# First stage of a Fourier mixer kernel: finer steps, a new hand-written order, fewer filler matmuls

## The chip, the cores and the metric

The kernel runs on one core of a Trainium2 chip. The metric is the device time of one execution in microseconds (us), the median of several runs. The core's engines are named as in the profile: PE (TensorE, matmuls), PEld (its weight loads), DVE (VectorE), ACT (ScalarE), POOL (GpSimd) and SP (SyncE, which here only issues DMAs).

## What is computed

Three layers, in 32-bit floats, for 4 batches of 768 rows with 512 columns:

```python
# 1. attention in chunks of 32 rows, 8 heads of 64, 8 memory keys beside a window of 56 keys
scores = scale * q_c @ k_full.T ; a = exp(scores - max) ; a = a / (sum(a) + 1e-9) ; out = a @ v_full
# 2. Fourier mixing and a dense layer
u  = x + real(fft(fft(x, axis=1), axis=2))
un = (u - mean(u)) / sqrt(var(u) + 1e-6)
x  = u + relu(un @ w_ch1) @ w_ch2              # 512 -> 2048 -> 512
# 3. gated convolution
h  = relu(x @ w_in)                            # 512 -> 1024
out = (h * sigmoid(conv3(h))) @ w_out          # 1024 -> 512
```

The weights come as 64-bit floats and are decoded on the chip to a high and a low 32-bit part; products of the large matrices are three matmuls each (high by high, high by low, low by high).

## The kernel before, in words

The program is one function whose steps are issued in an order that a string of letters, `SCHED` (L38), writes out by hand. A letter is one step, and `task` (L549) issues all its instructions on their engines at once; every engine then works through its own instructions in that order. `SCHED` has three parts, divided by `|`. Everything up to the end of part 3 is called the first stage here.

A *unit* is 96 rows of one batch, so there are 32 units, 8 to a batch. Its letters in part 1 are: `S` scores (L224, eight pairs of matmuls into the PSUM tile `sc`; then, in the same step, eight row maxima on DVE, `sm` and `ngm`, L240, and the load of the unit after next, L216); `E`, for half the heads, four exponentials on ACT (L248); `A`, for half the heads, four transposes on PE (`atp`, L257) and the copy out of PSUM (`at`, L163 or L161); `P` the product with the values (`o`, L268), then on DVE the denominators (`r`, L270, L271) and the scaled output (`xn`, L273), then on POOL the sums and differences of mirrored columns (`xf`, L278, L279); `X` four transposes on PE (`xtp`, L293) and the copy into the batch's rows `xT` (L296, L298). The scores use two PSUM buffers, one unit's worth, so the next unit's scores wait for this unit's row maxima.

`B` is one step of the Fourier transform of a batch (`dft`, L304), which can start when the batch's eight units are there: folding (`EO`, L309, L310, POOL; `F` and its high and low parts `Fhl`, L323 to L328), products with the tables (`z`, `p`, `pm` on PE), results `G` and `H` on DVE, their sum and difference `uc` (L462, L463), and the split into `uh` and `ul` (L477, L480). `D` is one step of the dense layer of a transformed batch (`dense`, L497): four of sixteen columns of the hidden layer, `h` (12 matmuls, L488; `hh` on ACT, `hl` on DVE), and the product `y` (12 matmuls, L507). `W` is one step of decoding a weight piece (`decode_all`, L105), mainly on DVE (`wsc`, `wlb`, `whb`). Which of two engines does a copy, a sum or a difference is written down for each instance in `ENGINES` (L39).

`F` is a filler: `keep(1)` (L204) multiplies a constant matrix with itself into a PSUM buffer that nobody reads (`idle`; one 32-bit product of 128 columns, which the profile counts as two matmuls).

The Fourier tables are loaded by POOL's queue in one go when the ninth `E` is issued (L563 to L566). After the first stage a loop of its own alternates `h` and `acc` products for the rest of the dense layer, then comes the third layer; neither is touched by the change apart from line numbers.

Of the kernel before, what the change touches and what calls it, by code (L numbers as in the profile page):

```python
# [37 lines left out]
SCHED = "FFFSEAEFSAWFWFFFEEPFFFSFFAFFWWAEPAFXSWFEAWESFFEWWPSFFEFFWXXAAEWWPEAFFSEFFFWAPAFFFEAXFEPAAFFFSFFFFFFWEFEXWPAASWXEWEPAXFFSFFBAPEEAXASFEBPSFAEBBFEFFFWBASEBXPXABASFEBWEBPAESFAWBBXBEPAAEESFBBBWBWXPASFBEABBWWBBBBXPEASFWXEAFFBWWPBEBEWASEBBAXEWPXAAFBSFEBBWEPSABBAWBWEXEDDWDWDPSAABEXDPDBBEBBBDABDAXESBBPDBEEBBXBABSDXBABPSEBBADBBABDPABDEBSEAXBBEBBEEPBSBABXBADBDEBBPEXABASDPBDADBDBBSXEXBDABESBPEABEABDBBSPBADFBBFEBXAEESDBBBBPABABBXDEPDBBAAEBXEBBBXBDBPADABDBPXDDXBB|BBBWDWBDWBBDWBDDDBBWWWBBWDDWBBBBWDWBWWDBDBWBWBWWWBWDWBWDDWWBWBBBWBBDBDBWDDBWBB|DDWDDWWDWWWWWDDWWWDWWHDWHDHDWHDWWWDDDWDWWWWWWW"  # L38
ENGINES = {'at': 'aaaaaaaaavavaaaaaaaaaaaaaaaaaaaaaaaaaaaaaaaaaavaaaavaaavaaaaaaaa', 'xt': 'vvvvaaaaaaaaaaaaavaaaaaaaaavaava', 'y': 'aaaaaaaaaaaaaaaaaaaaaaaaaaaaaaaa', 'uh': 'aaaaaaaaaaavavvvvaaavvaaavavaaaaaaaaaaavvv', 'ul': 'vvpvvvvvvvvvvvvpvvvvvvvvvpvvpppppvpvvvpppv', 'fl': 'pvvvvppvppvvppvp', 'f': 'vpvvvpppvpvpvvpv', 'u0': 'vvvvvvvv', 'u1': 'vvvvvvvv'}  # L39
# [7 lines left out]
def fourier_mixer_kernel(ctx: ExitStack, tc: tile.TileContext, qk, vw, w1, w2, w_in, w_out, conv_w,  # L47
# [57 lines left out]
    def decode_all(todo, st=None):  # L105

        st, lo_of = st or fetch(todo[0][0]), None
        for i, (_, where, f, spill) in enumerate(todo):
# [3 lines left out]
            while placed(f) is False:  # L112
                if lo_of is not None:
                    lo_of()
                    lo_of = None
                yield
# [51 lines left out]
    def run(gen, n=1):  # L168
        for _ in range(n):
            if next(gen, "end") == "end":  # L170
                return False
        return True
# [30 lines left out]

    def keep(n):  # L204

        p = ps_g.tile([128, 512], F32, tag="g", name="idle")
        for _ in range(n):
            mm(p[:, 0:128], onesm, onesm, start=True, stop=True)  # L208

    NUNITS = NB * NU  # L210
    units = {}
    def load_qk(u):
        if u < NUNITS:
            t = ldp.tile([128, QW + KWD], F32, tag="qk", name="qk", bufs=2)
            units[u] = {"qk": t}
            nc.sync.dma_start(out=t, in_=qk[u])  # L216

    def load_v(u):
        if u < NUNITS:
            t = ldp.tile([128, VW], F32, tag="vw", name="vw", bufs=3)  # L220
            nc.sync.dma_start(out=t, in_=vw[u])
            units[u]["vw"] = t

    def scores(u):  # L224
# [18 lines left out]
        d["ex"], d["ngm"] = sm, ngm  # L243
# [7 lines left out]
    def atr(u, half):  # L251
        d = units[u]
        if half == 0:
            d["at"] = smp.tile([128, NH, QB], F32, tag="at", name="at", bufs=1)
        at = ps_g.tile([128, 4, QB], F32, tag="g", name="atp")
        for i in range(4):
            nc.tensor.transpose(at[:, i, :], d["ex"][:, 4 * half + i, :], ident_sb[:QB, :QB])  # L257
        copy("at", d["at"][:, 4 * half:4 * half + 4, :], at)

    def pv(u):  # L260
# [3 lines left out]
        r = smp.tile([QB, NH], F32, tag="r", name="r")  # L264
        o = ps_o.tile([128, 2, 512], F32, tag="o", name="o")
        oh = o[:QB, :, 0:VW // 2].rearrange("p b (h e) -> p b h e", e=HD + 1)
        for h in range(NH):
            mm(oh[:, h // 4, h % 4, :], at_sb[:, h, :], vw[:, h * (HD + 1):(h + 1) * (HD + 1)], start=True, stop=True)  # L268
        r4 = r.rearrange("p (b h o) -> p b h o", b=2, o=1)
        nc.vector.tensor_scalar(out=r4, in0=oh[:, :, :, HD:HD + 1], scalar1=1e-9, scalar2=None, op0=ALU.add)  # L270
        nc.vector.reciprocal(out=r, in_=r)  # L271
        xn = smp.tile([QB, DM + 1], F32, tag="xn", name="xn", bufs=1)
        nc.vector.tensor_tensor(  # L273
            out=xn[:, 0:DM].rearrange("p (b h e) -> p b h e", b=2, e=HD), in0=oh[:, :, :, 0:HD],
            in1=r4.to_broadcast([QB, 2, 4, HD]), op=ALU.mult)
        xf = smp.tile([QB, 2, 256], F32, tag="xf", name="xf")
# [5 lines left out]
    xTs = {}  # L282

    def xtr(u):
        d = units.pop(u)
        b, blk = divmod(u, NU)
        if blk == 0:
            xTs[b] = xtp.tile([128, 4, S + 1], F32, tag="xT", name="xT")
        xT = xTs[b]
        xf = d["xf"].rearrange("p a (m c) -> p (a m) c", c=128)  # L290
        p = ps_g.tile([128, 4, QB], F32, tag="g", name="xtp")
        for i in range(4):
            nc.tensor.transpose(p[:, i, :], xf[:, i, :], ident_sb[:QB, :QB])  # L293
# [10 lines left out]
    def dft(b):  # L304
# [3 lines left out]
        for sl, rv in ((slice(97, 385), slice(671, 383, -1)), (slice(0, 97), slice(768, 671, -1))):  # L308
# [3 lines left out]
            while NU * b + NU - 1 in units or count["X"] < NU * b + NU:  # L312
                yield "wait"
# [20 lines left out]
        def zstep(c, m):  # L334
# [5 lines left out]
            z = ps_g.tile([128, 512], F32, tag="g", name="z")  # L340
# [9 lines left out]
            accumulate(z[:sn, 0:nw], seq)  # L350
            zh = dfp.tile([97, 256], F32R, tag=f"zh{c % 2}{m}", name="zh")
# [6 lines left out]
            if c < 2:  # L358
                nc.vector.tensor_tensor(out=zn[:sn, 1], in0=z[:sn, 256:258], in1=zn[:sn, 0].bitcast(F32),
                                        op=ALU.subtract)  # L360
                ZN[c, m] = zn
            Z[c, m] = (zh, zl, sn)

        def part(c, n, zc):
            terms = []
# [53 lines left out]
        def center(hf, gs):  # L419
            ss = slice(hf * HALF, hf * HALF + HALF)  # L420
            pm = ps_g.tile([128, 512], F32, tag="g", name="pm")
            mm(pm[:, 0:HALF], onesm, gs, start=True, stop=True)  # L422
            for m in range(2):
                nc.vector.tensor_tensor(out=G[:, m, ss], in0=G[:, m, ss], in1=pm[:, 0:HALF], op=ALU.subtract)
            nc.scalar.copy(gs[0:1, :], pm[0:1, 0:HALF])
            nc.sync.dma_start(out=mud[b][:, ss], in_=gs[0:1, :])

        gs = summed(0)
        for c in (2, 3):
            for m in range(2):  # L430
# [6 lines left out]
        for m in range(2):  # L437
            zc = slice(128 * m, 128 * m + 128)
            p = ps_g.tile([128, 512], F32, tag="g", name="p")
            for c, o, n in ((2, 0, 194), (3, 256, 192)):  # L440
# [4 lines left out]
                accumulate(p[:, o:o + n], seq[-1:], start=False)  # L445
            pj = p.rearrange("p (r j) -> p j r", r=2)
# [11 lines left out]
            yield  # L458
        uc = dfp.tile([128, 4, S], F32, tag="Fhl", name="uc")
        for hf in range(2):  # L460
# [5 lines left out]
            yield  # L466
            yield from split_uc(2 * b + hf, uc[:, :, ss])
            if hf:
                bgb.append(dense(b))
# [14 lines left out]
    def g1(c, f):  # L484
        uh, ul = uhl[c]
        need(("1", f))
        p = ps_g.tile([128, 512], F32, tag="g", name="h")
        accumulate(p[:, 0:TC], split3([(w1h[f][:, k * 128:k * 128 + 128], w1l[f][:, k * 128:k * 128 + 128],  # L488
                                        uh[:, k], ul[:, k]) for k in range(4)]))
        hh = a1p.tile([128, TC], F32R, tag="hh", name="hh", bufs=NI)  # L490
# [542 lines left out]
```

## Time and profile before

| what | us |
|---|---|
| median of 3 runs (1019.08 to 1025.03) | 1019.93 |
| the profiled execution, whole | 1020.89 |
| its span, from first to last instruction | 1018.1 |
| first stage ends (first `acc` product) | about 348 |

The span is what the profile's rows cover; the profiled execution's own time is 2.8 us longer than its span. Rows of the profile give the busy time of engines, the waits, and the instructions in order of time; times in them count from the span's start.

### The profile page before, as it was taken

To read this page: it belongs to the slowest core of one execution; us is meant where nothing else is said; L and a number is where in the kernel's file an instruction comes from. 1 tells how busy PE (TensorE), PEld (TensorE's weight loads), DVE (VectorE), ACT (ScalarE), POOL (GpSimd) and SP (SyncE) were. 2 spreads that over 40 slices of the span, in tenths; PEclk is the share of its full clock that TensorE was granted. 3 is DMA by queue.
4 is the path that set the end of the run, shared out by engine and by line. 5 is a ranking of instruction groups with operands and counts; after the bars stand their busy time and mean duration, and the time that the engine had idled before them with its cause. 6 is when DMAs were issued, how large, how long until landed. Compare 5 with 4: busy or idle time off the path is not lost.

```text
span 1018.1 us, 16674 instructions
## 1 busy us (share of the span) xinstructions
PE 999.1 (98%) x6430; PEld 957.6 (94%) x6430; DVE 685.8 (67%) x1508; ACT 442.5 (43%) x923; POOL 214.9 (21%) x232
## 2 busy tenths in 40 slices
PE   7899999999999999999999999999999999999997
PEld 6888989999999999999999999999999999999996
DVE  4889956766988775767787775635357566465554
ACT  4687754664444423333333332212245454454442
POOL 1353251422400000102211000202013222222222
PEclk9999999999999999999999999999999999999999
DMA  6864532522437545575788972818543111010101
GB/s 198 264 185 138 182 105 78 164 72 81 129 100 235 179 152 194 187 182 125 174 201 224 199 183 83 148 49 164 159 123 115 52 69 56 1 62 1 62 1 62
DMA packets 63807, 130.86 MB, mean 129 GB/s; under 512 B 4919, under 2 KB 39199, under 8 KB 63503
## 3 DMA queue, kind: packets, MB, share of 16 engines
q1 hardware_dynamic: 51424, 102.35, 30.6%
q0 software_dynamic: 12048, 27.17, 14.9%
q8 instruction: 50, 0.82, 0.3%
q14 instruction: 29, 0.24, 0.1%
q10 hardware_dynamic: 256, 0.28, 0.1%
HBM read 92.28 MB, written 43.79 MB: 134 GB/s over the span
## 4 chain that ended last, share of the span: by engine, by line
PE 90%; DVE 5%; issue 2%; ACT 1%; DMA 1%; POOL 1%; DVEq 0%; POOLq 0%; ACTq 0%
PE acc L66 32%; PE h L66 25%; PE ph L66 12%; PE y L66 6%; PE o L268 3%; PE sc L234 2%; PE p L66 2%; PE z L66 2%; DVE sm L240 2%; PE atp L257 2%; PE idle L208 1%; PE xtp L293 1%; PE pm L422 1%; ACT sm L248 0%; DMA qk<-in_qk 0%
## 5 line engine op out<-in xcount | busy, mean ns | idle before, releaser
L66 PE MATMUL acc<-hh,w 128*128 128x384 f32 x768 | 208.0, 334 | 0.0
L66 PE MATMUL h<-uh,w 128*128 128x384 f32 x768 | 208.0, 334 | 0.0
L492 ACT ACTIVATE hh<-h 128x384 fp32r<-128x384 f32 x128 | 62.5, 490 | 247.2 <-PE h L66 247.1
L493 DVE SCALAR_TENSOR_TENSOR hl<-h,hh 128x384 fp32r<-128x384 f32 x128 | 70.5, 554 | 145.6 <-ACT hh L492 145.1
L66 PEld LDWEIGHTS acc<-hh,w 128*128 128x128 f32 x768 | 139.8, 188 | 0.0
L66 PEld LDWEIGHTS h<-uh,w 128*128 128x128 f32 x768 | 139.8, 188 | 0.0
L66 PE MATMUL ph<-xh,wit 128*128 128x384 f32 x512 | 136.3, 337 | 0.7 <-ACT hrow L823 0.7
L66 PE MATMUL acc<-hl,w 128*128 128x384 f32 x384 | 128.3, 334 | 0.0
L66 PE MATMUL h<-ul,w 128*128 128x384 f32 x384 | 128.3, 334 | 0.0
L66 PE MATMUL acc<-wot,hgh 128*128 128x512 f32 x384 | 119.6, 393 | 0.0
L831 DVE SCALAR_TENSOR_TENSOR cv<-hrow,cw_sb,cv 128x768 f32<-128x768 f32 x64 | 110.1, 1721 | 3.1 <-ACT cv L825 2.0
L843 POOL TENSOR_TENSOR hgl<-cv,hgh 128x768 fp32r<-128x768 f32 x32 | 60.4, 1886 | 194.6 <-ACT hgh L842 179.0
L837 DVE TENSOR_TENSOR cv<-hrow,cv 128x768 f32<-128x768 f32 x32 | 30.7, 959 | 99.2 <-ACT cv L836 99.1
L66 PEld LDWEIGHTS ph<-xh,wit 128*128 128x128 f32 x512 | 93.3, 188 | 2.6 <-ACT hrow L823 1.4
L66 PE MATMUL ph<-xl,wit 128*128 128x384 f32 x256 | 86.1, 336 | 0.0
L66 PEld LDWEIGHTS acc<-wot,hgh 128*128 128x128 f32 x384 | 71.7, 188 | 13.4
L248 ACT ACTIVATE sm<-sm,ngm 96x128 f32<-96x128 f32 x256 | 80.5, 394 | 7.4 <-DVE ngm L240 7.4
L823 ACT ACTIVATE hrow<-ph 128x384 f32<-128x384 f32 x64 | 31.3, 493 | 102.3 <-PE ph L66 101.1
L66 PE MATMUL acc<-wot,hgl 128*128 128x512 f32 x192 | 74.7, 389 | 0.0
L66 PEld LDWEIGHTS acc<-hl,w 128*128 128x128 f32 x384 | 72.1, 188 | 0.0
L66 PEld LDWEIGHTS h<-ul,w 128*128 128x128 f32 x384 | 72.1, 188 | 0.0
L240 DVE CUSTOM_DVE_ANT_0 sm<-sc,mask_sb 96x128 f32<-96x128 f32 x256 | 56.3, 282 | 18.3 <-PE sc L234 14.5
(150 smaller groups left out, 1879.2 us busy)
## 6 DMA issues: line engine op xcount, KB each, us to landing
w<-in_w SPq DMA_DIRECT2D x32, 512.0 KB, 4.1
qk<-in_qk SPq DMA_DIRECT2D x32, 448.0 KB, 3.5
us<-ucd SPq DMA_DIRECT2D x13, 768.0 KB, 7.9
yp<-yd SPq DMA_DIRECT2D x13, 768.0 KB, 8.4
vw<-in_vw SPq DMA_DIRECT2D x32, 260.0 KB, 3.0
ucd<-uc SPq DMA_DIRECT2D x8, 768.0 KB, 4.7
yd<-y SPq DMA_DIRECT2D x32, 192.0 KB, 2.0
ucd<-mud POOLq DMA_DIRECT2D x8, 768.0 KB, 14.4
```

The costliest lines, as they stand in the source:

```text
L66: mm(o, a, b, start=(start and i == 0), stop=(stop and i == n - 1))
L234: mm(sch[2 * a + g], qT[64 * g:64 * g + 64, a, :], kT[64 * g:64 * g + 64, a, :], start=True, stop=True)
L240: nc.vector.tensor_tensor_reduce(out=sm[:, h, :], in0=sch[h], in1=mask_sb[:, kind, :], op0=ALU.add, op1=ALU.min, scale=-0.125, scalar=3e38 ...
L248: nc.scalar.activation(out=d["ex"][:, h, :], in_=d["ex"][:, h, :], func=AF.Exp, scale=-1.0, bias=d["ngm"][:, h:h + 1])
L257: nc.tensor.transpose(at[:, i, :], d["ex"][:, 4 * half + i, :], ident_sb[:QB, :QB])
L268: mm(oh[:, h // 4, h % 4, :], at_sb[:, h, :], vw[:, h * (HD + 1):(h + 1) * (HD + 1)], start=True, stop=True)
L492: nc.scalar.activation(out=hh, in_=p[:, 0:TC], func=AF.Relu)
L493: nc.vector.scalar_tensor_tensor(out=hl, in0=p[:, 0:TC], scalar=0.0, in1=hh.bitcast(F32), op0=ALU.max, op1=ALU.subtract)
L823: nc.scalar.activation(out=h[:, 1 + hf * TC:1 + hf * TC + TC], in_=p[:, 0:TC], func=AF.Relu)
L831: nc.vector.scalar_tensor_tensor(out=cv, in0=h[:, j:j + S], scalar=cw_sb[:, j, f:f + 1], in1=cv, op0=ALU.mult, op1=ALU.add)
L837: nc.vector.tensor_tensor(out=cv, in0=h[:, 1:S + 1], in1=cv, op=ALU.mult)
L843: nc.gpsimd.tensor_tensor(out=hgl[i], in0=cv, in1=hgh[i].bitcast(F32), op=ALU.subtract)
```

## The change

Steps are cut finer, and the string is written anew. The row maxima become a step of their own in two halves (`T`); the copies out of PSUM are steps apart from the transposes (`a`, `x`); the denominators, the reciprocal and the scaled output are steps of their own (`p`, `r`, `n`); each load of a unit is a step (`l`, `v`); the tables come in five pieces (`t`). A `B` or `D` step is cut in two where its product has been issued and its result has not been read. `SCHED` has 13 `F` where it had 63, and 34, 24 and 29 `W` in its three parts where it had 33, 27 and 26. `ENGINES` is written anew as well. The assertions (`after`, `bank`, `taken`, `spent`) issue nothing, and `AHEAD` is empty.

```diff
-SCHED = "FFFSEAEFSAWFWFFFEEPFFFSFFAFFWWAEPAFXSWFEAWESFFEWWP
...
+SCHED = "FFWFvSTETSAlEWWlTATvWEaaWSTPEEAFaTApWSarEFlnPT
...
 def load_qk(u):
-        if u < NUNITS:
-            t = ldp.tile([128, QW + KWD], F32, tag="qk", name="qk", bufs=2)
...
+    def load_table(n):
+
+        if n in (0, 1):
+            nc.gpsimd.dma_start(out=dtab_sb[:, n], in_=dtab[:, n])
+        elif n == 2:
+            nc.sync.dma_start(out=sgn_sb, in_=sgn)
+            for row in (0, LOROW):
+                nc.gpsimd.dma_start(out=orow_sb[row:row + 1], in_=orow)
+        else:
+            nc.gpsimd.dma_start(out=stab_sb[:, n - 3], in_=stab[:, n - 3])
...
+    def rowmax(u, half):
...
-        for h in range(NH):
+        for h in range(4 * half, 4 * half + 4):
             nc.vector.tensor_tensor_reduce(
...
+    def denom(u):
...
         nc.vector.tensor_scalar(out=r4, in0=oh[:, :, :, HD:HD + 1], scalar1=1e-9, scalar2=None, op0=ALU.add)
+
+    def inverse(u):
+        r = units[u]["r"]
         nc.vector.reciprocal(out=r, in_=r)
+
+    def pv_out(u):
...
     def dense(b):
...
-                g1(c, f)
+                p = g1(c, f)
+                if f == NI - 1:
+                    spent_u.add(c)
+                yield "half"
+                g1_out(c, f, p)
                 yield
...
-            if n == 8:
-                nc.gpsimd.dma_start(out=dtab_sb, in_=dtab)
-                for row in (0, LOROW):
-                    nc.gpsimd.dma_start(out=orow_sb[row:row + 1], in_=orow)
-                nc.gpsimd.dma_start(out=stab_sb, in_=stab)
...
+        elif k == "T":
+            rowmax(n // 2, n % 2)
```

Three places show what moves. On PE at the start of the program, before (`sc` scores, `atp` and `xtp` transposes, `o` the product with the values, `idle` the fillers):

```order
L208 MATMUL idle<-onesm 128x128 x3
L234 MATMUL sc<-qk 96x128 x8
L257 MATMUL atp<-ident_sb,sm 128x96 x4
L208 MATMUL idle<-onesm 128x128
L234 MATMUL sc<-qk 96x128 x8
L257 MATMUL atp<-ident_sb,sm 128x96 x4
L208 MATMUL idle<-onesm 128x128 x4
L268 MATMUL o<-vw,at 96x65 x8
L208 MATMUL idle<-onesm 128x128 x3
```

and on PE at the same place in the changed kernel:

```order
L227 MATMUL idle<-onesm 128x128 x3
L281 MATMUL sc<-qk 96x128 x16
L315 MATMUL atp<-ident_sb,sm 128x96 x8
L281 MATMUL sc<-qk 96x128 x8
L331 MATMUL o<-vw,at 96x65 x8
L315 MATMUL atp<-ident_sb,sm 128x96 x4
L227 MATMUL idle<-onesm 128x128
```

The second unit's scores now stand ahead of the first unit's transposes, the third unit's ahead of the first product with the values, and of the eleven fillers of the first list four are left.

On DVE where the first unit's output is scaled, before (`r` denominators, `xn` the output, `wlb`, `wsc` and `rxb` the decoding of weights):

```order
L125 TENSOR_SCALAR wlb<-w_153 128x512
L129 SCALAR_TENSOR_TENSOR wlb<-w_153,wlb 128x512
L270 TENSOR_SCALAR r<-o 96x8
L271 RECIPROCAL r<-r 96x8
L273 TENSOR_TENSOR xn<-o,r 96x512
```

and on DVE at that place in the changed kernel:

```order
L340 TENSOR_SCALAR r<-o 96x8
L145 SCALAR_TENSOR_TENSOR rxb<-wlb,wsc 128x512
L129 TENSOR_SCALAR wsc<-w_204 128x512
L130 TENSOR_SCALAR wlb<-w_204 128x512
L344 RECIPROCAL r<-r 96x8
L351 TENSOR_TENSOR xn<-o,r 96x512
```

Weight steps now stand between the parts of what was one step.

On POOL where batch 0's transform ends (`gs` a sum of two halves of `G`, `xf` a unit's mirrored sums), before:

```order
L279 TENSOR_TENSOR xf<-xn 96x256
L416 TENSOR_TENSOR gs<-G 128x384 x2
L277 COPY xn<-xn 96x1
L278 TENSOR_TENSOR xf<-xn 96x256
L279 TENSOR_TENSOR xf<-xn 96x256
```

and on POOL at that place in the changed kernel:

```order
L509 TENSOR_TENSOR gs<-G 128x384
L356 COPY xn<-xn 96x1
L357 TENSOR_TENSOR xf<-xn 96x256
L358 TENSOR_TENSOR xf<-xn 96x256
L171 TENSOR_TENSOR uc<-G,H 128x2x384 x2
```

The two sums `uc` of the first half of batch 0, which DVE made before, are POOL's now, behind the mirrored sums of other units.

## Rows read from the trace of the kernel before

**Rows 1.** The page: busy time of each engine; PE's busy tenths in 40 slices

```profile
PE 999.1 (98%) x6430; PEld 957.6 (94%) x6430; DVE 685.8 (67%) x1508; ACT 442.5 (43%) x923; POOL 214.9 (21%) x232
...
PE   7899999999999999999999999999999999999997
```

**Rows 2.** Windows: stretch, length, PE, PEld, DVE, ACT, POOL busy (instructions), clock, DMA share, GB/s

```profile
0.00:60.20 60.20, 51.13 (x501) 45.79 (x502) 40.66 (x219) 37.21 (x106) 17.38 (x35) 1.00 0.73 226
60.20:117.80 57.60, 55.17 (x584) 50.25 (x583) 53.11 (x244) 45.05 (x134) 21.85 (x36) 1.00 0.53 159
117.80:348.00 230.20, 228.64 (x1720) 222.46 (x1719) 175.57 (x497) 117.50 (x297) 63.49 (x80) 1.00 0.38 124
348.00:1018.00 670.00, 664.21 (x3633) 639.11 (x3631) 416.45 (x550) 242.71 (x389) 112.19 (x82) 1.00 0.46 119
```

**Rows 3.** Windows of the fillers alone (tile idle): PE busy, PEld busy

```profile
0.00:60.20 60.20, 16.20 (x92) 13.40 (x92) 1.00 0.73 226
60.20:117.80 57.60, 6.04 (x30) 4.18 (x30) 1.00 0.53 159
117.80:348.00 230.20, 0.77 (x4) 0.67 (x4) 1.00 0.38 124
```

**Rows 4.** Timeline of PE: start us, length us, instruction, idle before it

```profile
1.09 1.65 PE L208 MATMUL idle<-onesm 128*128 128x128 f32 x6 [1.09 <-DVE expl L76]
5.05 2.02 PE L234 MATMUL sc<-qk 64*96 64x128 f32 x16 [2.31 <-DMA qk<-in_qk]
...
15.91 1.12 PE L234 MATMUL sc<-qk 64*96 64x128 f32 x16
...
47.73 1.83 PE L208 MATMUL idle<-onesm 128*128 128x128 f32 x14
49.40 0.49 PE L293 MATMUL xtp<-ident_sb,xf 96*128 96x96 f32 x4
...
60.18 0.49 PE L293 MATMUL xtp<-ident_sb,xf 96*128 96x96 f32 x4
...
117.78 0.42 PE L66 MATMUL h<-uh,rxa 128*128 128x384 f32 x1
```

**Rows 5.** Waits of DVE up to 117.8 us: total us, times, longest

```profile
DVE sm L240 <- PE sc L234: 13.4, 7, 6.1
DVE r L270 <- PE o L268: 4.6, 5, 1.6
```

**Rows 6.** Timeline of DVE: start us, length us, instruction, idle before it

```profile
7.10 0.29 DVE L240 CUSTOM_DVE_ANT_0 sm<-sc,mask_sb 96x128 f32<-96x128 f32 x1 [6.05 <-PE sc L234]
7.32 0.28 DVE L240 CUSTOM_DVE_ANT_0 sm<-sc,mask_sb 96x128 f32<-96x128 f32 x1
...
123.27 2.50 DVE L129 SCALAR_TENSOR_TENSOR wlb<-w,wlb 128x512 int32<-128x512 int32 x1
```

**Rows 7.** Groups of instructions by line: busy us, mean ns of one, idle before

```profile
L129 DVE SCALAR_TENSOR_TENSOR wlb<-w,wlb 128x512 int32<-128x512 int32 x48 | 36.1, 752 | 0.6
...
L166 POOL TENSOR_TENSOR ul<-us,uh 128x768 fp32r<-128x768 f32 x10 | 20.5, 2057 | 138.4 <-ACT uh L163 94.1 <-DVE uh L161 44.3
...
L166 DVE TENSOR_TENSOR uc<-G,H 128x768 f32<-128x768 f32 x16 | 14.5, 947 | 0.0
...
L166 POOL TENSOR_TENSOR F<-EO 128x576 f32<-128x576 f32 (+2 forms) x7 | 8.5, 1208 | 0.0
L166 POOL TENSOR_TENSOR Fhl<-F,Fhl 128x386 fp32r<-128x386 f32 (+1 forms) x8 | 8.4, 1055 | 19.4 <-ACT Fhl L325 19.4
L166 DVE TENSOR_TENSOR F<-EO 128x579 f32<-128x579 f32 (+3 forms) x9 | 8.3, 924 | 4.1 <-POOL EO L309 4.1
...
L166 DVE TENSOR_TENSOR Fhl<-F,Fhl 128x384 fp32r<-128x384 f32 (+1 forms) x8 | 5.0, 625 | 1.2 <-ACT Fhl L325 1.1
...
L296 DVE TENSOR_SCALAR xT<-xtp 128x384 f32<-128x384 f32 x7 | 3.8, 549 | 0.0
```

**Rows 8.** Timeline of POOL: start us, length us, instruction

```profile
123.39 1.84 POOL L166 TENSOR_TENSOR ul<-uc,uh 128x768 fp32r<-128x768 f32 x1
```

More of the change, by code (lines that the diff above doesn't have):

```diff
@@ L166, in either, with run @@
         (nc.vector if vector(what) else nc.gpsimd).tensor_tensor(out=out, in0=in0, in1=in1, op=op)
[L168 to L172, printed above, removed]
+    def run(gen):
+        return next(gen, "end") not in ("end", "wait")
     def rxt(tag, name):
@@ L202, in fourier_mixer_kernel, with bank, taken, after @@
     sgn_sb = cst.tile([128, 1], F32, name="sgn_sb")
+    banks = []
+    def bank(name):
+        i = len(banks) - PSG
+        assert i < 0 or banks[i][1], "the bank's last product is still unread"
+        t = ps_g.tile([128, 512], F32, tag="g", name=name)
+        banks.append([t, False])
+        return t
+    def taken(*tiles):
+        for entry in banks[-PSG:]:
+            entry[1] |= any(entry[0] is t for t in tiles)
+    def after(k, n):
+        assert count[k] >= n, "a step comes before the last reader of its buffer"
     def keep(n):
-        p = ps_g.tile([128, 512], F32, tag="g", name="idle")
+        p = bank("idle")
+        taken(p)
         for _ in range(n):
@@ L282, in fourier_mixer_kernel, with xtr_out @@
     xTs = {}
+    spent, spent_u = set(), set()
     def xtr(u):
-        d = units.pop(u)
+        d = units[u]
+        xf = d["xf"].rearrange("p a (m c) -> p (a m) c", c=128)
+        p = d["xtp"] = bank("xtp")
+        p = p[:, 0:4 * QB].rearrange("p (a q) -> p a q", a=4)
+        for i in range(4):
+            nc.tensor.transpose(p[:, i, :], xf[:, i, :], ident_sb[:QB, :QB])
+    def xtr_out(u):
+        xp = units.pop(u)["xtp"]
+        p = xp[:, 0:4 * QB].rearrange("p (a q) -> p a q", a=4)
+        taken(xp)
         b, blk = divmod(u, NU)
         if blk == 0:
+            assert b < 2 or b - 2 in spent, "the rows before last are still read"
             xTs[b] = xtp.tile([128, 4, S + 1], F32, tag="xT", name="xT")
         xT = xTs[b]
[L290 to L293, printed above, removed]
         xo = xT[:, :, blk * QB:(blk + 1) * QB]
@@ L339, in zstep @@
             nw = CW if c < 2 else SW
-            z = ps_g.tile([128, 512], F32, tag="g", name="z")
+            after("t", 3)
+            z = bank("z")
             terms = []
@@ L466, in dft @@
             yield
+            assert b == 0 or 2 * b + hf - 2 in spent_u, "the chunk before last is still read"
             yield from split_uc(2 * b + hf, uc[:, :, ss])
             if hf:
-                bgb.append(dense(b))
+                split_done.add(b)
             yield
@@ L533, in fourier_mixer_kernel, with all_dft, all_dense @@
     wit = []
-    bga, bgb = [], []
-    def step_of(q):
-        moved = False
-        while q:
-            got = next(q[0], "end")
-            if got != "end":
-                return moved or got != "wait"
-            q.pop(0)
-            moved = True
-        return moved
-    count = dict.fromkeys("SEAPXW", 0)
+    def all_dft():
+        for b in range(NB):
+            while count["x"] < NU * b + NU - 1:
+                yield "wait"
+            yield from dft(b)
+    def all_dense():
+        for b in range(NB):
+            while b not in split_done:
+                yield "wait"
+            yield from dense(b)
+    split_done = set()
+    count = dict.fromkeys("lvtSTEAaPprnXxWBDH", 0)
     todo = {}
```

168 lines of the change are left out of this document (116 added, 52 removed).

## The prediction

> **What bounds the kernel now.** I read the page first [rows 1]: PE is busy for 98% of the span, so a shorter time has to come out of PE's idle time or out of PE's work that computes nothing. The slices show where the idle time is: at the beginning. Then I cut the span at marks of PE's timeline [rows 4]: 60.2 us, where the eighth unit is transposed and batch 0 is complete; 117.8 us, where the first dense product `h` starts, behind the first Fourier transform; 348 us, the end of the first stage. The windows [rows 2] give PE's idle time: 9.1 us before the first mark, 2.4 up to the second, 1.6 up to the third. From the second mark on PE is the bound of the first stage. The fillers [rows 3] are 92, 30 and 4 matmuls, so 46, 15 and 2 fillers. Seven of them in a row took from 47.73 to 49.40 us [rows 4], 0.24 us each. So ahead of 117.8 us PE spends 11.5 us idle and 61 x 0.24 = 14.6 us on fillers, 26 us in all, and behind it 2.1 us.
>
> What PE lacks there comes mostly from DVE, which is busy for 40.7 + 53.1 = 93.8 of the 117.8 us [rows 2] and starts its first row maximum only at 7.10 us [rows 6]. From there it is idle for 17.3 us (110.7 less 93.4), and its waits name the other side [rows 5]: 13.4 us for scores (6.1 of these are the start) and 4.6 us for the product with the values. PE and DVE wait for each other in turn, since a step's row maxima stand directly behind its scores.
>
> **The change, part by part.** Everything hangs on when the first `h` can start, because the work behind it only shifts. I work that out from both engines.
>
> PE. By the order, 13 fillers are left, 8 before the eighth unit, 5 more before the first `h`, none after. Taking 48 out ahead of `h` is worth at most 48 x 0.24 = 11.5 us; it makes room, and is a gain only if the next product is ready. PE's busy time ahead of `h`, 51.1 + 55.2 = 106.3 us, less 14.6 of fillers is 91.7. One unit's scores more stand ahead of `h` (22 for 21 units, 1.1 us), 13 fillers cost 3.1, and the wait before the first scores, 1.1 + 2.3 us [rows 4], stays. That makes 99.3 us, with no other wait at all.
>
> DVE. Counted in the order up to the first `ul`, the changed kernel has 8 row maxima more (160 to 168, 0.22 us each by their starts at 7.10 and 7.32 [rows 6]: +1.8), 3 `xT` fewer (0.55), 2 `F` fewer (0.92), 2 `Fhl` fewer (0.63) and 2 `uc` fewer (0.95) [rows 7]: -1.6 - 1.8 - 1.3 - 1.9. The weight steps ahead of it are the same. The sum is -4.8, so DVE needs 93.4 - 4.8 = 88.6 us behind its start at 7.1: 95.7 us without any wait.
>
> What DVE gives up, POOL takes: two `F` of 1.21, two `Fhl` of 1.06 and two `uc`, for which no row on POOL exists. The nearest, a difference of the same size, is 2.06 [rows 7]. That is 8.6 us more on POOL, whose 39 of 118 us leave room [rows 2]. But it can hold DVE up. At 123.27 us a weight step took 2.50 us [rows 6] where its line's mean is 0.75 [rows 7], and POOL's `ul` of 1.84 us lay across it [rows 8]. So the bounds are 0 and 8.6 us. I take 3, about a third: the line's mean of 0.75 over 48 instructions leaves room for few as long as this one. [...]
>
> DVE's waits. Of the 17.3 us, 7.3 are for scores behind the first ones. Weight steps now stand between scores and row maxima, and the halves let one unit's transposes go while the other half is still computed, so I expect most of that to go. The 4.6 us for the product with the values should halve, as other work stands between its parts. The remaining 5.4 us are short. Bounds are 0 and 17.3; I take 5. Then the first `h` starts at 95.7 + 3 + 5 = 103.7, say 104 us. PE would then have 4.7 us of waits above its 99.3, where it has 8.1 above the start now. What is late next is DVE, which decides the start of `h` in this sum.
>
> Loads. The tables go in five pieces, between the first unit and the eleventh. The DMA engines are busy for 73% of the first 60.2 us [rows 2], or 44 us, and about the same bytes (the second table's second half less) have to land in the 50 us that I expect up to the eighth unit. They fit, with less room. The load of a unit waits in SP's queue behind the release of its buffer, as before, so I cost this at nothing; if that cover goes, a late load costs PE a wait like the 2.3 us for the first one [rows 4], which is inside the range.
>
> Behind the first `h`. The work is the same: 8 products `h` and 8 `y` for each of four batches, ten units left instead of eleven, weight steps 34 + 24 + 29 for 33 + 27 + 26. PE loses one unit's scores (1.1 us) and two fillers (0.5), and has 1.6 us of waits that may go or stay. DVE is busy for 175.6 of 230.2 us there and hides the alternation of weight and dense steps; it would need over 50 us more to become the bound. `ENGINES` gives it 27 copies more there (about 0.55 each by `xT` [rows 7], +15) and takes some 14 differences and sums away (5 `uc`, 5 `ul`, 2 `F`, 2 `Fhl`, -13), and these 14 on POOL, 25 us by the prices above, could hold it for no more than that. I take -1.5 us, between -3 and +3. The stages behind 348 us are untouched.
>
> Sum, against the profiled execution: 1020.9 - (117.8 - 104) - 1.5 = 1005.6 us. That execution lies 1.0 above the median, so the forecast is 1005 us for the median (1.5% faster). Its own range goes from the first `h` at 97 us (just under PE's own sum, in which some busy time is restart after waits) with -3 behind it, 996, to the first `h` at 109 us, 1010.
>
> **The rivals.**
> The waits stay. The fillers stood where PE had nothing ready; without them the same time is idle. For it: DVE has little spare time, 53.1 of 57.6 us busy in the second window, and the last of its work decides. Against it: DVE's idle time is named, and comes from the order of steps. If all 17.3 us stay, the first `h` is at 95.7 + 17.3 + 3 = 116 us, the gain 1.8 + 1.5, and the median 1016.6, say 1017.
>
> POOL holds DVE. All 8.6 us are paid, and the waits stay: 121.6 us for the first `h`, 3.8 later than now, less 1.5 behind it: 1022. For it speaks the held row, against it that most rows of that line are not.
>
> [...]
>
> **How the numbers follow.** Forecast 0.70, waits stay 0.20, POOL 0.03, clock 0.07. One per cent, 10.2 us, is about what a measurement of this kernel can tell from no change: faster means under 1009.7, slower over 1030.1. The forecast's range lies on the faster side almost whole, the waits and POOL within it, the clock beyond: faster 0.70, same 0.23, slower 0.07. The range of 8 in 10 reaches from 996 to the case of staying waits, 1017.
>
> **What would show it.** Right: the first `h` near 104 us; fillers of 26 matmuls; DVE's wait for scores down to its start and a few us; PE idle below 5 us between the first scores and `h`; the stretch from first `h` to first `acc` 227 to 231 us; the pace of score matmuls 1.1 us a unit from 15 to 20 us on. Wrong: the eighth unit later than 55 us, or the first `h` later than 109; long two-input instructions on DVE beside POOL's `uc` and `F`; score matmuls of 2 us behind 25 us; PE waiting for `hl` or weights behind the first `h`.

## The result and the profile after

The changed kernel takes 1007.43 us (median of 4 runs, 1005.59 to 1008.38) against 1019.94. The ratio is 0.9865, 95% interval 0.9829 to 0.9901: 1.3% faster, 12.5 us. The profiled execution took 1008.38 us, with a span of 1006.6.

First the page of the changed kernel, its busy times and PE's slices, which answer to [rows 1]:

```profile
PE 990.3 (98%) x6330; PEld 949.6 (94%) x6330; DVE 682.6 (68%) x1515; ACT 432.8 (43%) x896; POOL 251.5 (25%) x254
...
PE   7999999999999999999999999999999999999998
```

PE has 100 matmuls and 8.8 us less (50 fillers of two matmuls), POOL 36.6 us more. The windows, cut at the same marks as [rows 2] (eighth unit transposed, first `h`, first `acc`; columns as there), and under them two short stretches to which the text comes further down:

```profile
0.00:51.00 51.00, 44.63 (x437) 40.25 (x438) 37.24 (x221) 38.67 (x112) 18.51 (x36) 1.00 0.80 251
51.00:106.20 55.20, 52.98 (x567) 48.73 (x566) 50.85 (x249) 44.49 (x131) 33.84 (x43) 0.97 0.56 179
106.20:338.00 231.80, 228.74 (x1702) 221.73 (x1700) 177.09 (x499) 107.63 (x267) 87.66 (x94) 0.99 0.38 125
338.00:1006.60 668.60, 663.95 (x3632) 638.86 (x3630) 417.43 (x548) 242.05 (x388) 111.44 (x82) 1.00 0.46 118
...
66.80:70.20 3.40, 3.40 (x27) 2.90 (x26) 2.49 (x13) 3.17 (x9) 2.71 (x4) 0.50 0.04 12
121.40:124.80 3.40, 3.40 (x22) 3.12 (x19) 1.01 (x2) 3.40 (x12) 0.00 (x0) 0.50 0.16 58
```

The eighth unit is transposed at 51.0 us for 60.2, the first `h` starts at 106.2 for 117.8. Up to `h` PE is idle for 8.6 us (106.2 less 44.63 and 52.98), where it was 11.5. Behind `h` nothing is gained: by the exact starts, first `h` to first `acc` took 232.2 us for 230.9, the rest 668.2 for 669.5. So the account of the profiled executions is -11.5 + 1.3 - 1.3, and -1.0 around the span: 12.5 us. The first `acc` on PE, before and after:

```profile
348.63 0.34 PE L66 MATMUL acc<-hh,w 128*128 128x384 f32 x1
...
338.39 0.33 PE L67 MATMUL acc<-hh,w 128*128 128x384 f32 x1
```

The timeline of PE, as [rows 4]:

```profile
5.32 2.02 PE L281 MATMUL sc<-qk 64*96 64x128 f32 x16 [2.58 <-DMA qk<-in_qk]
...
19.33 2.03 PE L281 MATMUL sc<-qk 64*96 64x128 f32 x16
24.24 1.12 PE L281 MATMUL sc<-qk 64*96 64x128 f32 x16
...
50.99 0.50 PE L370 MATMUL xtp<-ident_sb,xf 96*128 96x96 f32 x4
...
65.00 1.57 PE L331 MATMUL o<-vw,at 128*96 128x65 f32 x16 [1.97 <-DVE xn L351]
...
106.24 0.42 PE L67 MATMUL h<-uh,rxa 128*128 128x384 f32 x1
...
120.26 0.45 PE L67 MATMUL y<-hl,rxc 128*128 128x384 f32 x1 [1.93 <-DVE hl L595]
```

Score matmuls of 2.03 us a unit still run at 19.33, where [rows 4] have 1.12 at 15.91: the pace rose later. And two waits of 1.97 and 1.93 us are new, at 65.0 and 120.3. Behind each stands one of the two short windows above. The granted clock is 0.50 there, one or two us behind the end of each wait. The trace's record of the granted clock begins only where the pace rises, with 1.00 at 13.5 us in the profiled execution of before and at 22.4 here; ahead of that the windows' column reads 1.00 though a unit's scores take 2 us. Where it begins is called the clock's rise below; the slow pace ahead of that and the stretches at 0.50 are the lower level. Before, no window from the rise to 1017 us shows 0.50.

What PE waited for is seen on DVE and POOL. DVE's timeline, columns as in [rows 6]:

```profile
62.33 1.52 DVE L130 TENSOR_SCALAR wlb<-w 128x512 int32<-128x512 int32 x1
...
64.26 0.69 DVE L351 TENSOR_TENSOR xn<-o,r 96x512 f32<-96x512 f32 x1
...
115.83 3.90 DVE L145 SCALAR_TENSOR_TENSOR rxd<-wlb,wsc 128x512 fp32r<-128x512 int32 x1
119.66 0.54 DVE L595 SCALAR_TENSOR_TENSOR hl<-h,hh 128x384 fp32r<-128x384 f32 x1
```

POOL's timeline over the same two places, as [rows 8]:

```profile
62.54 1.01 POOL L171 TENSOR_TENSOR Fhl<-F,Fhl 128x384 fp32r<-128x384 f32 x1
...
115.85 0.19 POOL L387 COPY xT<-xT 128x4 f32<-128x4 f32 x1
116.00 1.92 POOL L396 TENSOR_TENSOR EO<-xT 128x864 f32<-128x864 f32 x1
117.88 1.31 POOL L397 TENSOR_TENSOR EO<-xT 128x576 f32<-128x576 f32 x1
119.14 1.22 POOL L396 TENSOR_TENSOR EO<-xT 128x291 f32<-128x291 f32 x1
```

`rxd` takes 3.90 us; the same instruction took 0.68 in the run below in which the folding comes later. By its end (119.73, less 0.68) it came through at about 119.05, where POOL's second `EO` ends and the third starts. The `hl` that PE wants is queued behind it. At 62.33 a `wlb` of 1.52 us, where the median of its line in this run is 0.42, lies across a POOL instruction in the same way, and `xn` behind it is what PE waits for at 65.0.

DVE's waits up to 110 us, beside [rows 5]:

```profile
DVE sm L296 <- PE sc L281: 10.3, 6, 6.3
DVE r L340 <- PE o L331: 3.1, 7, 1.2
```

Behind the start (6.3) DVE waits 4.0 us for scores, where it was 7.3, and 3.1 for the product with the values, where it was 4.6.

### The profile page after: what moved, and what is told of

Read it like the earlier page. It is cut to its first block, busy times and chain, and to the rows that moved or that the text cites. A ratio compares the mean times of both kernels' runs of the same rounds, so it can differ in the third digit from the quotient of the medians.

```text
span 1006.6 us, 16470 instructions
## 1 busy us (share of the span) xinstructions
PE 990.3 (98%) x6330; PEld 949.6 (94%) x6330; DVE 682.6 (68%) x1515; ACT 432.8 (43%) x896; POOL 251.5 (25%) x254
## 4 chain that ended last, share of the span: by engine, by line
PE 90%; DVE 6%; ACT 2%; DMA 1%; POOL 1%; issue 1%; DVEq 0%; POOLq 0%
PE acc L67 33%; PE h L67 25%; PE ph L67 13%; PE y L67 6%; PE o L331 3%; PE sc L281 3%; PE z L67 2%; PE p L67 2%; PE atp L315 2%; DVE sm L296 1%; PE xtp L370 1%; ACT sm L303 1%; PE pm L515 1%; DVE uc L171 1%; DVE ul L171 0%
## 5 line engine op out<-in xcount | busy, mean ns | idle before, releaser
L594 ACT ACTIVATE hh<-h 128x384 fp32r<-128x384 f32 x128 | 62.5, 490 | 249.9 <-PE h L67 249.8
L67 PEld LDWEIGHTS acc<-wot,hgh 128*128 128x128 f32 x384 | 71.7, 188 | 13.4
```

The lines of the kernel that those rows point to most:

```text
L67: mm(o, a, b, start=(start and i == 0), stop=(stop and i == n - 1))
L594: nc.scalar.activation(out=hh, in_=p[:, 0:TC], func=AF.Relu)
```

## The experiments

My theory was that the gain comes from the order and its finer steps, which close the waits between PE and DVE; that the missing fillers give nothing by themselves; and that part of the gain is given back by a late rise of the clock, and by DVE instructions that POOL holds. The rivals: fillers or loads or the table of engines are the gain. Each run stood beside the kernel before on the same chip (1019.50 to 1019.74 us); ratios are to that.

**The fillers alone.** The kernel before, with only its first 13 fillers:

```diff
-SCHED = "FFFSEAEFSAWFWFFFEEPFFFSFFAFFWWAEPAFXSWF...
+SCHED = "FFFSEAEFSAWFWFFFEEPFFFSFFAWWAEPAXSW...
```

> The kernel before, with its first 13 fillers kept and the 50 later ones left out; order and steps are the old ones. If the gain is the time of the fillers themselves (50 x 0.24 us), it comes here too: 1007 to 1009 us. If the fillers stood where PE had nothing ready, and the gain is that of the new order, the waits stay: 1015 to 1020 us, first h at 114 us or later, and DVE's wait for scores up to there still above 12 us. [...]

1022.21 us, ratio 1.0021 (1.0001 to 1.0042). In its profile `h` starts at 124.9 us, and DVE waits 15.6 us for scores and 6.8 for the product with the values, where it was 13.4 and 4.6. Two of its four stretches with the clock at 0.50, by the windows (the others are 10.2 us from 43.3 and 3.4 from 101.3):

```profile
26.20:39.80 13.60, 13.14 (x84) 11.50 (x84) 10.86 (x49) 10.36 (x31) 4.80 (x10) 0.50 0.83 267
...
70.60:80.80 10.20, 10.20 (x69) 9.18 (x69) 7.01 (x27) 7.32 (x21) 4.41 (x6) 0.50 0.40 138
```

So in the old order the fillers bought the clock (37.4 us at 0.50 here, none in the profiled execution of before), and leaving them out gains nothing. They do cost time where the clock is equal: two of this kernel's ten runs had a mean granted clock of 0.995 and took 1018.5 and 1018.7 us, and eleven of the 60 executions of the kernel before that stood beside the experiments had 0.995 too and took 1023.6 to 1024.1. So the lower level comes back in some runs of the kernel before as well.

**More and fewer fillers in the new order.** Eight more in the first units, and only the first three:

```diff
-SCHED = "FFWFvSTETSAlEWWlTATvWEaaWSTPEEAFaTApWSar...
+SCHED = "FFWFvSTETFFFFSAlEWWlTATvWEaaWSTFFFFPEEAFaTApWSar...
```

> The changed kernel with eight fillers more: four ahead of the second unit's scores, where PE waited 1.65 us, and four ahead of the first product with the values. In the changed kernel score matmuls keep the slow pace (2.0 us a unit) up to 22 us, in the kernel before up to 13.5. If the missing early fillers are what delays the level's rise, the pace changes at 12 to 16 us here, the first h comes 1 to 3 us earlier than its 106.2 us, and the time is 1004 to 1006.5 us. If the late rise has another cause, the fillers only cost: 1008 to 1010 us and the pace changes at 20 us or later.

```diff
-SCHED = "FFWFvSTETSAlEWWlTATvWEaaWSTPEEAFaTApWSarEFlnP...
+SCHED = "FFWFvSTETSAlEWWlTATvWEaaWSTPEEAaTApWSarElnP...
```

> The changed kernel with its first three fillers only, the ten others left out. If fillers cost their time, 10 x 0.24 us come off: 1005 us. [...] If they are room that nothing else fills, 1007 to 1008.

1004.88 us, ratio 0.9846 (0.9821 to 0.9871), and 1008.33, ratio 0.988 (0.9846 to 0.9914). The intervals overlap with the change's. With eight more the clock rises at 9.3 us, `h` starts at 103.4, and the clock is 0.5 for 6.8 and 3.4 us later on; with three it rises at 12.8, but is 0.5 for 13.7 us from 60.6 and for 3.4 from 122.1, and `h` starts at 106.4. The rise at 12.8 is not the work of the missing fillers: up to 18 us PE's order is the same as in the change, which rose at 22.4. The number of fillers doesn't decide: these three kernels lie within 3.5 us, and the old order with 13 fillers is 14 us above the slowest of them.

**Whole steps in the new order.** Row maxima both at the first half's place, the copies `at` out of PSUM directly behind their transposes, the division in one piece at its last letter (the old order has it at `P`); loads, tables, `x` and the halves of `B` and `D` stay as in the change:

```diff
         elif k == "T":
-            rowmax(n // 2, n % 2)
+            if n % 2 == 0:
+                rowmax(n // 2, 0)
+                rowmax(n // 2, 1)
...
-        elif k == "p":
-            denom(n)
...
         elif k == "n":
+            denom(n)
+            inverse(n)
             pv_out(n)
```

> The changed kernel's order, but the halves are joined again: both row maxima at the even half, a unit's copies out of PSUM directly behind its transposes, and the division's three parts at the last. Theory: finer steps let DVE work while the second half of a unit is still computed, so without them DVE waits longer for scores (from 4.0 us behind the start back to 6 or more) and `h` comes 3 to 6 us later: 1010 to 1014 us. Rival (the order of whole steps, weights between dense ones, is the gain, and the halves are detail): within 2 us of 1007.4.

1023.35 us, ratio 1.0012 (0.9992 to 1.0033): the whole gain is gone, more than I expected. Four of its twelve runs, the profiled one among them, took 1017.0 to 1017.5 us with a mean granted clock of 0.996 or 0.997, and six took 1023.3 to 1023.8 with 0.990. So at about the clock of the changed kernel (0.996 to 0.998) 10 us are lost, and the rest goes with the clock. In the profiled run `h` comes 4.4 us later, as expected, though DVE's waits for scores behind the start are 4.9 us and not 6 or more, and h to acc takes 4.6 us longer, which I had not expected. PE's waits behind `h`:

```profile
PE y L67 <- DVE hl L595: 2.5, 1, 2.5
PE p L67 <- DVE zl L446: 1.6, 2, 1.4
PE h L67 <- DVE zn L448: 1.4, 1, 1.4
PE o L331 <- DVE xn L351: 1.4, 2, 0.7
```

These are 6.9 us, where the changed kernel's waits there are 3.1 (1.9 + 0.7 + 0.5). Finer steps are not a detail of this order. The old order with its whole steps was about as fast as this one, so the new order alone does not gain, and steps and order together do. What finer steps gain in the old order was not run.

**The tables in one go.** All pieces at the third one's place:

```diff
-        if n in (0, 1):
-            nc.gpsimd.dma_start(out=dtab_sb[:, n], in_=dtab[:, n])
-        elif n == 2:
+        if n == 2:
             nc.sync.dma_start(out=sgn_sb, in_=sgn)
+            nc.gpsimd.dma_start(out=dtab_sb, in_=dtab)
...
-        else:
-            nc.gpsimd.dma_start(out=stab_sb[:, n - 3], in_=stab[:, n - 3])
+            nc.gpsimd.dma_start(out=stab_sb, in_=stab)
```

> The changed kernel with the five pieces of the tables loaded in one go at the third piece's place. Theory: the pieces cost and give nothing, since the tables are wanted only from the first transform on: 1007 to 1008 us, `h` within 1 us of 106.2. Rival: the pieces keep the loads of the units from queueing behind 2 MB or more; in one go the units' loads come late, PE shows waits for DMA of 1 us or more in the first 50 us, and `h` comes 2 us or more later: 1009.5 or more.

1015.18 us, ratio 0.995 (0.9933 to 0.9967): 7.8 us slower than the change, the rival. The timeline of PE has one row for it:

```profile
43.05 2.02 PE L279 MATMUL sc<-qk 64*96 64x128 f32 x16 [6.94 <-DMA qk<-in_qk]
```

2.2 MB of tables are issued from 28.0 us on, a unit's load stands beside them, and PE waits 6.94 us for it; the clock is 0.5 for 6.8 us from 40.3 and for 10.2 from 71.0, the eighth unit comes at 56.5, and `h` at 114.7. In the kernel before the same single go, from 33.3 us, made no wait for `qk` but the first: its units came slower.

**The old table of engines.** `f`, `fl`, `u0`, `u1` and `ul` as before the change, so DVE keeps what went to POOL:

```diff
...
-'f': 'pvpppppvvppvvppp', 'u0': 'pvpppvpv', 'u1': 'pvvvvpvv'}
+'f': 'vpvvvpppvpvpvvpv', 'u0': 'vvvvvvvv', 'u1': 'vvvvvvvv'}
```

> The changed kernel with the kernel before's table for the differences and sums (`f`, `fl`, `u0`, `u1`, `ul`), so DVE does those that the change gave to POOL; order, steps and copies stay. My theory (the order's gain, with DVE as the partner that decides): DVE gets some 4 us more work ahead of the first `h` (two `F` 1.8, two `Fhl` 1.3, and `uc` 1.9, less what POOL's hold gives back), so `h` comes 2 to 5 us later, at 108 to 111, and behind `h` DVE has room, so h to acc stays within 230 to 233; 1009 to 1013 us. Rival A (POOL's holds cost as much as they take off DVE): `h` within 1 us of 106.2, and with fewer POOL runs the 1.9 us wait for `hl` behind `h` goes too: 1005 to 1008. Rival B (half of the gain came from this table): 1014 us or more.

1009.17 us, ratio 0.9886 (0.9863 to 0.9909), in the range of my theory, though the intervals overlap. `h` starts at 111.5, 5.3 us later, and h to acc takes 229.6, 2.5 us less: the wait of 1.9 us for `hl` is gone. DVE is busy for 94.6 us up to `h`, 6.5 more than in the change. But the clock is also at the lower level there for 12.5 us behind its rise (at 20.5), where the change has 3.4:

```profile
64.90:71.70 6.80, 6.80 (x48) 6.30 (x47) 5.17 (x33) 4.33 (x12) 3.26 (x5) 0.50 0.23 57
105.80:112.60 6.80, 6.80 (x45) 6.30 (x44) 6.77 (x23) 4.14 (x13) 1.21 (x2) 0.50 0.49 157
```

The three of its six runs with a mean clock of 0.997 or 0.998 took 1006.1 to 1007.5 us, as the change did at 0.996 to 0.998 (1005.6 to 1008.4). So a gain from the work given to POOL is not shown.

**Two weight steps ahead of POOL's folding,** to get `rxd` out of POOL's way:

```diff
-vSXBWDDDTxlTDDDPvDWDADB
+vSXWWBDDDTxlTDDDPvDDADB
```

> The changed kernel with the last two weight steps of its first weights (DVE's wsc and rxd) moved ahead of the split of batch 0's second half, so that rxd no longer meets POOL's folding of batch 1, beside which it took 3.9 us instead of 0.7; PE waited 1.9 us for the hl behind it and the clock fell for 3.4 us after. If POOL's hold on DVE caused that wait and that fall, both go and the time falls by 1.5 to 4 us: 1003.5 to 1006. If DVE is simply late there, the wait stays or another takes its place: 1007 to 1008.5.

1011.55 us, ratio 0.9902 (0.9882 to 0.9923), slower than the change, against what I expected. The hold found another victim. DVE's timeline:

```profile
111.62 7.24 DVE L171 TENSOR_TENSOR ul<-uc,uh 128x768 fp32r<-128x768 f32 x1
118.78 0.54 DVE L595 SCALAR_TENSOR_TENSOR hl<-h,hh 128x384 fp32r<-128x384 f32 x1
```

POOL worked without a gap from 111.10 to 120.00, and this `ul` (0.95 us where nothing holds it) came through only behind six of its instructions. PE waited 4.15 us for `hl`, and the clock was 0.5 for 6.8 us. Behind the wait at 65.5 us, 1.98 us here, it did not fall in this run.

**POOL's folding later,** a dozen steps, with the weight step where the change has it:

```diff
-vDWDADBpSrXBAaDEaDnED
+vDWDADpSrXAaDEaDnBBED
```

> The changed kernel with the two steps that fold batch 1's even and odd parts (three POOL instructions of 1.92, 1.31 and 1.22 us in one run at 116.0) moved behind the next unit's division, a dozen steps later. Theory (a DVE instruction with two SBUF inputs that meets POOL's unbroken run is held to about its end): the `rxd` at about 115.8 takes under 1 us for 3.90, PE's wait of 1.9 us for `hl` at 120.3 goes, the granted clock doesn't fall to 0.5 at 121.4, and h to acc is 2 to 4 us shorter than 232.2: 1003.5 to 1006 us. Rival A (the hold moves to another DVE instruction at the new place, as it did with the weight step placed early): PE's wait of 1.5 us or more turns up 3 to 10 us later, with or without a fall; 1006 to 1009 us. Rival B (the fall has nothing to do with the wait): the wait goes and the fall stays.

1005.96 us, ratio 0.9849 (0.9827 to 0.9871), on the border of my theory and rival A. `rxd` took 0.68 us and its wait is gone, but another wait turned up 10 us later, as rival A has it, though not by its reason: no DVE instruction was held, POOL itself was late for the next unit. The largest of PE's waits behind `h`:

```profile
PE xtp L370 <- POOL xf L357: 2.5, 1, 2.5
```

The clock stayed up at 121 us and was 0.5 for 6.8 us from 131.6, behind that wait; h to acc took 233.8.

**Two weight steps moved, POOL left alone:**

```diff
-FBBWAXFAEaxBtESvBFnBTXTBalPEp
+FBBAXFAEaxBtESvBFnBTXTBalPWEp
...
-vDWDADBpSrXBAaDE
+vDDADBpSrXBAaWDE
```

> The changed kernel with two weight steps moved by a few places: one (its `wlb` of 1.5 us delayed `xn`, for which PE waited 1.97 us at 65.0) behind the next unit's products, one (its `rxd` of 3.9 us delayed `hl`, for which PE waited 1.93 us at 120.3) behind the third `hl`. POOL's work and its order stay. Theory (a DVE instruction is held by POOL's unbroken run, PE waits for what stands behind it, and a fall of the granted clock follows each such wait): both waits go, no 0.5 between 25 us and the end in the run with a profile, `h` at 103.5 to 105, h to acc 229 to 231: 1002.5 to 1004.5 us. Rival A (as with the fold moved later: the time shows up in another wait of 1.5 us or more soon behind): 1005.5 to 1008. Rival B (the falls come by themselves): the waits go and a fall stays in 55 to 75 or 115 to 135 us.

1003.23 us (1001.40 to 1009.53), ratio 0.9843 (0.9814 to 0.9872). At 120 us it went half as my theory had it: `rxd` is still held (2.49 us), and PE waits for it, but only 1.3 us; no fall follows, and h to acc takes 229.7 for 232.2. At 65 us rival A came true: PE still waits 1.79 us, since the moved step now delays the next unit's `xn`, and the clock is 0.5 for 3.4 us. `h` at 102.6 is early also because the clock rose at 14.6 us in this run; five others with this beginning, the change among them, had 20.5 to 23.3, and the run with three fillers 12.8.

**The same, with the eight fillers more:**

> The same two weight steps moved, and the eight fillers more in the first units of the earlier run (its 1004.9 us had the clock's rise at 9.3 us for 22.4, and both waits). Theory: the two gains add, `h` at 101 to 103, h to acc 229 to 231: 1000 to 1002.5 us. Rival (with the clock up early the fillers only fill waits that are there anyway): within 1 us of the run without them.

1001.72 us (999.56 to 1003.56), ratio 0.9815 (0.9793 to 0.9837): the best of all, 5.7 us under the change, though the two intervals overlap by a little. Against the run without the eight fillers (1003.23) they overlap for the most part, so what the fillers add is not shown. `h` starts at 103.9 in the profiled run, which has 6.8 us at 0.5 and is the slowest of the five.

**Fillers in the wait that is left.** The same kernel with a step that issues fillers ahead of the product which waits at 62.5 us:

```diff
-alPWEpAxAranaSPBWETA
+alPWEpAxAranaSKPBWETA
...
+        elif k == "K":
+            keep(14)
```

> The kernel with two weight steps moved and eight fillers more (1001.7 us; PE waits 1.78 us at 62.5 and the granted clock is 0.5 from 64.6 to 71.5), with 14 filler matmuls, some 1.7 us by those of this case (two in 0.24 us), put between the scores and the product that waits there. They compute nothing. Theory (the fall of the clock follows PE's wait): PE's wait there shrinks below 0.5 us, the clock is 1.00 between 50 and 80 us, and as the fillers only fill the wait, `h` comes some 3 us earlier (half of 6.8), at 100 to 102; 998 to 1001 us. Rival A (the fall comes whatever PE does there): 0.5 stays in 60 to 75 us, 1001.5 to 1003. Rival B (the fillers are late themselves and push the product back by their own time): 1003 us or more.

1001.96 us (1001.24 to 1002.07), ratio 0.9823 (0.9804 to 0.9841). One filler is two matmuls, so 28 ran, twice what I wanted. `h` starts at 102.7, and the time is outside the 998 to 1001 of my theory. PE's timeline:

```profile
63.11 3.39 PE L227 MATMUL idle<-onesm 128*128 128x128 f32 x28
66.34 0.90 PE L331 MATMUL o<-vw,at 128*96 128x65 f32 x9
```

The windows from the clock's rise on:

```profile
11.70:300.00 288.30, 284.46 (x2516) 271.05 (x2515) 229.34 (x886) 170.39 (x470) 139.65 (x167) 1.00 0.45 148
300.00:997.00 697.00, 695.42 (x3813) 670.42 (x3811) 447.42 (x605) 257.44 (x416) 111.35 (x82) 1.00 0.46 122
```

No stretch at 0.5 is left, which speaks for the theory that the fall needs a wait ahead of it. The time is not better: the product starts 3.2 us behind its scores, where it was 1.8. All five runs took 1001.2 to 1002.1 us at a mean granted clock of 0.999 or 1.000. Without these fillers two runs had 1.000 too, and took 999.6 and 1000.2, and the one at 0.996 took 1003.6. So the fillers cost some 1.4 us by the trace (3.2 less 1.8) and 2 by these times, and with them no fall came in five runs; without them it comes in some runs and not in others.

**Weight steps in fours,** in parts two and three of the order, part one left as it is:

```diff
-|DDBDBWBWBDDBDWBBDBDBWBBBDB...
+|DDBDBBBDDBDBBDBDBWWWWBBBDB...
```

> The changed kernel with the weight steps behind the first stage (parts two and three of the order) bunched in fours at the place of each fourth, the first stage as it is. Theory: what follows the first stage has DVE far from being the bound, so this is within 1 us of 1007.4, and the stretch from the first `acc` to the end, 668.2 us, changes by less than 1.5. Rival: four weight steps in a row (each some 2 us of DVE) delay a dense copy, PE waits, and that stretch gets 3 us or more longer: 1010.5 or more.

1020.46 us, ratio 0.9992 (0.9973 to 1.0012): 13 us lost (7 to 9 in its two runs with a mean clock of 0.998), the rival, and at another place than I wrote. Parts two and three lie ahead of the first `acc`, and h to acc takes 244.4 us. The largest wait, on PE's timeline:

```profile
311.95 0.69 PE L67 MATMUL h<-uh,rxa 128*128 128x384 f32 x1 [4.74 <-DVE hl L595]
```

DVE's timeline ahead of it has the weight steps in a row, the `hl` behind them:

```profile
305.72 1.95 DVE L129 TENSOR_SCALAR wsc<-w 128x512 int32<-128x512 int32 x1
...
308.65 0.68 DVE L137 SCALAR_TENSOR_TENSOR whb<-w,wsc 128x512 int32<-128x512 int32 x1
309.37 0.43 DVE L141 TENSOR_SCALAR wsc<-whb 128x512 int32<-128x512 int32 x1
310.41 1.49 DVE L595 SCALAR_TENSOR_TENSOR hl<-h,hh 128x384 fp32r<-128x384 f32 x3 [0.61 <-ACT hh L594]
```

The row of weight steps is not all of it. The line of the `wsc` of 1.95 us has a median of 0.43 in the changed kernel, and an instruction of POOL lay across it here:

```profile
305.23 2.15 POOL L171 TENSOR_TENSOR ul<-uc,uh 128x768 fp32r<-128x768 f32 x1 [5.01 <-PE h L67]
```

And the windows show two stretches at 0.50, which I estimate at 3.4 us lost in the first (half of PE's 6.76) and 2.1 in the second (half of 4.15):

```profile
268.30:275.10 6.80, 6.76 (x30) 6.62 (x29) 3.19 (x11) 0.75 (x3) 0.86 (x1) 0.50 0.08 29
309.30:316.10 6.80, 4.15 (x13) 4.15 (x14) 2.08 (x6) 1.77 (x4) 0.00 (x0) 0.50 0.48 182
```

The beginning of this run is that of the change, and it has the same two waits, 1.88 us at 64.5 and 1.93 at 118.2, but no fall behind either. The second on PE's timeline, and the window behind it:

```profile
118.22 0.44 PE L67 MATMUL y<-hl,rxc 128*128 128x384 f32 x1 [1.93 <-DVE hl L595]
...
118.20:125.00 6.80, 6.78 (x62) 6.37 (x63) 3.66 (x15) 4.40 (x15) 3.56 (x6) 1.00 0.17 60
```

## Why the prediction was right, and where not

The time was right to 2.4 us (1005 for 1007.4), and the main line of it too: the gain lies ahead of the first `h`, 11.5 us where I had 13.8. It comes about half from PE's and DVE's waits for each other: DVE's idle time behind its start fell from 17.2 to 11.0 us, and its busy time up to `h` from 93.5 to 87.9. That the start of `h` came so near is in part luck, since two terms of DVE's sum were wrong in opposite directions. By its steps:

- PE's sum: the eighth unit at 51.0 us for a forecast 50; fillers 26 matmuls, as forecast (16 before the mark at 51.0 and 10 behind it). Between the first scores and `h` PE is idle for 4.9 us (8.6 less the first 1.1 and 2.6), just below the 5 that I had named.
- DVE's sum: it started at 7.37 and was busy for 87.9 us from there to `h`, holds included. I had 88.6 and 3 for POOL, 3.7 too much. The step that failed here is this 3: summed over the instructions that took longer than their kind does, DVE was held for 2.1 us ahead of `h`, and 1.8 before, so 0.3 more. The other 1.0 lies in the count of its work.
- DVE's waits: I took 5 us; they are 11.0 (106.24 - 7.37 - 87.89). Less went than I had expected, and this is the larger error. The errors are -3.7 here above, +6.0 in this step, and 0.3 for the start, unrounded 2.5 together, so 103.7 + 2.5 = 106.2.
- POOL's prices: two `uc` took 3.6 us on POOL for my 4.1. But where POOL holds DVE counts for more than how long it works: the costliest hold (3.90 us) lies behind `h`, and I had put the price of POOL ahead of it.
- Behind `h` I had -1.5 and got +1.3. PE did lose a unit's scores and two fillers, 1.6 us; the fall at 121.4 took some 1.7 of it back (half of 3.4 us at 0.50, an estimate), and PE's idle time rose from 1.6 to 3.1, most of it the wait for `hl`.
- The loads were costed at nothing, with "less room", and in pieces they cost nothing: PE waits for `qk` only at the start. But the cover that I named (DMA engines with room on the mean) does not explain it, since the same bytes in one go cost 7.8 us: there PE waited 6.94 us for one unit's load, due while 2.2 MB of tables were under way.
- That DVE "hides the alternation of weight and dense steps", as its 175.6 of 230.2 us leave room, was the wrong kind of reason. The same work in fours costs 13 us.

The rivals: the waits did not all stay, and POOL held DVE ahead of `h` for little more than before, though one such hold, the `wlb` at 62.33, stands ahead of PE's wait at 65.0. The clock, my rival for the slower side (0.07), is real but smaller: it rose at 22.4 us instead of 13.5, which I estimate at 4 us at most (8.9 us of work at 2.03 us for a unit's scores that take 1.12 later), and the falls at 66.8 and 121.4 at 1.7 each (half of 3.4, by the granted 0.50). That it could take the time over 1030 us was my estimate, and no execution of the changed kernel shows it: the four took 1005.59 to 1008.38 us at a mean granted clock of 0.996 to 0.998. In the old order without the fillers it did decide: 37.4 us at 0.50, and no gain. In the new order PE has work at hand instead. Two signs of being wrong that I had named did show: score matmuls of 2.03 us behind 25 us (at 67.44, in the first fall), and PE waiting for `hl` behind `h`.

What stays open: why the clock rises at 12.8 and 14.6 us in two runs and at 20.5 to 23.3 in five others with the same beginning, and why a wait brings a fall in some runs only. In the profiled runs of the new order, from the clock's rise to the first `acc`, PE has 22 waits of 1.5 us or more; 17 have a fall with them or behind them, and five, of 1.71 to 2.49 us, have none. Their length does not decide it: the wait of 1.93 us for `hl` has a fall behind it in the change and none in the run with weight steps in fours. As the falls differ from run to run, the times of the experiments hold them too, and differences of a few us between them can't be told from that. The 1.3 us that the rest of the program gained was not followed up.

## What to carry to other kernels

Filler work was worth here what it did to the clock (without 50 fillers the old order had 37.4 us at 0.50 and gained nothing), so take it out only together with an order that gives the engine real work in its place, and look for falls of the granted clock behind each wait that is left (17 of 22 had one). Compare variants at the same mean granted clock. An engine with a quarter of its time free still delayed its partner by 4.74 us where several long steps stood in a row ahead of the one that was waited for: alternate them. And where a second engine takes work off the first, look at what lies beside its longest unbroken run (here a `ul` of 7.24 us for 0.95).

## What the runs showed of the hardware

Two DVE instructions between SBUF tiles that met a run of POOL instructions were held over more than one of them: `rxd` took 3.90 us for 0.68, and `ul` 7.24 for 0.95, each until about a boundary between two POOL instructions (by its end less its own time, 119.05 where POOL's next starts at 119.14, and 117.91 for 118.00). POOL's `EO` beside which it then ran took 1.22 and 1.48 us, for 0.77 in the run with the folding later; there a copy of POOL took 0.71 us, for 0.19 in the change, beside an `rxd` of 0.68. Instructions with one input were longer beside POOL too: `wlb` 1.52 us for 0.42, `wsc` 1.95 for 0.43. Moving the held `rxd` moved the hold to the `ul` of 7.24 us, or shortened it to 2.49, as long as POOL's run stayed in place.

A granted clock of 0.50 came back with or behind 17 of 22 waits of 1.5 to 6.9 us in the new order, whose PE is busy for 98% of the span, for 3.4 or 6.8 us in most cases (13.7 at most), and did not behind five of 1.71 to 2.49 us. In the old order with 13 fillers it came back behind waits of 0.9 and 1.1 us too (at 70.6 and 26.2). With the wait at 62.5 us filled, none of five runs showed it (mean clock 0.999 or 1.000). So a wait can cost this kernel more than its own length: in the change each of the two stretches at 0.50 holds 3.40 us of PE's work, and I estimate half of it, 1.7 us, as lost.
